# Row tile 11's normalised rows into a query-row buffer, and a new table of halved projections

## The chip, the core and the metric

The kernel runs on one core of a Trainium2 chip. The core has a matrix engine (PE, whose weight loads the profile lists apart as PEld), a vector engine (DVE), an activation engine (ACT), a general engine (POOL) and a queue engine (SP) that issues DMAs; POOL issues DMAs too. Each engine works through its own instructions in order and waits on semaphores for the others. Data lies in DRAM, in an on-chip buffer of 128 partitions (SBUF) and in the accumulators of the matrix engine (PSUM).

The metric is device time in microseconds (us) of one execution. The kernel before took 1621.09 us (median of 3 runs, 1619.76 to 1622.24).

## What is computed

Two layers, each applied twice in turn to the same 2048 rows of 512 values: a recurrent attention with a memory (A) and a gated mixer (B).

```python
x = x + A(layernorm(x)); x = x + B(layernorm(x))     # and both once more

# A: 64 segments of 32 rows, one after the other
h = concatenate([mem, xs])                 # 8 memory rows + 32 rows
q, k, v = h @ Wq, h @ Wk, h @ Wv           # 32 heads of 128
o = softmax(mask(q @ k.T * scale)) @ v @ Wo
mem = o[:8]                                # goes into the next segment
# B: over all 2048 rows
z = gelu(x @ w_in)                         # 1376 columns
g = w_sp @ layernorm(z[:, 688:]) + b_sp
out = (z[:, :688] * g) @ w_out
```

A segment needs the memory of the segment before it, so the 64 segments of a layer form one chain.

## The kernel before

**Blocks and segments.** The outer loop runs two blocks; each is `a_block` (64 segments, four to a row tile of 128 rows, 16 row tiles) and then `b_block`. `segment(s, ...)` issues one segment. On PE it holds, in this order: the projections of q and k in two halves each (`qk`, L929 and after), those of v (`v_mm`), the scores, the sums, the product with v, and the output projection with Wo (`wo_pairs`, L798; `wo_rest`, L805). Calls of `fill()` between them put in work that hangs on no recent result: the projections of the next row tile's last rows (`b_units`) or parts of an output projection (`y_part`, L817). A segment begins when DVE has written the new memory into the transposed rows `hT` (L907).

**Projections and their halving.** `mm_chunk` (L708 to L723) issues a projection of 512 columns as four contraction steps (`kt`) of four matmuls, one for each group of 32 partitions, each with its own weight load: 16 matmuls and 16 loads. While the counter `halve[0]` is above zero, a step with `kt > 0` is issued as two matmuls of 256 columns in place of one of 512, so 8 PE instructions more (4 loads and 4 matmuls), and the counter goes down by one. `segment` sets the counter behind the third q/k projection from the digit of `HALVED` that belongs to this block and segment (0 to 9); the fourth q/k projection and the two of v then use it up. What is computed stays the same. PE reads its program from DRAM in pieces, which the profile counts as the queue of instructions.

**Who orders what.** PE, DVE and ACT run in the order in which the code issues. The order on POOL in `a_block`, and that of SP there, is settled by a planner; in `b_block` SP is fixed as well and POOL is planned.

**The end of the attention.** Rows that have both their attention output and their residual are summed (`y_add`), their mean and variance taken (`y_stats`), and normalised by `y_norm` (L245 to L250): one DVE operation writes 512 bfloat16 columns into a buffer, and a DMA on SP stores it to `xb_d`, from which B loads transposed rows. Without a buffer as argument `y_norm` takes a tile `ln_xn`, a name with two buffers: the third user waits until the store that read the first has landed. At the end of `a_block` (L1260 to L1281) the row tiles 9 (in the last segment's `tail`), 10 and 11 are normalised one after the other (with `NB` = 16, `NB - 6` is 10 and `NB - 5` is 11). DVE's next operations are the two sums of `o_end` (L1277), the last attention output, stored by POOL (L1279) and SP (L1281).

**The start of the mixer.** `b_block` projects 16 row tiles (`project`, L296), with an activation on ACT (L297) and statistics on DVE (L300). DVE also adds the attention output to the row tiles 12 to 15 (`late_sum`, L228; its operands come by POOL, L222 and L224), takes their factors (`norms`) and normalises them (`late_norm`, L249). The first two of these take `ln_xn` again. POOL stores them to `xb_d` (L250), and SP loads them transposed (`load_rows`, L184) for `project(12)` and after. Then follow the 16 steps of the mixing product (L396) and of the output projection (L439), PE work throughout.

**The buffers of the query rows.** `segment` holds the projected q and k rows in tiles `rows` of the tag `rowsQK`, three buffers in the pool `rowp`; ACT writes them (L932), DVE transposes them (L935). Behind the last segment's transposes they lie idle. The pool ends with `a_block`, and its memory goes to tiles of `b_block`.

Of the kernel before, what the change touches and what calls it, by code (L numbers as in the profile page):

```python
# [7 lines left out]
BF16 = mybir.dt.bfloat16  # L8
# [6 lines left out]
P = 128  # L15
DM = 512
# [12 lines left out]
WO_PAIR = 18  # L29
LATE_STATS = 14  # L30
HALVED = (
    "5392919491949293909080707080708070807080708070708070807070807190",
    "8093929293929060070807070807080708070708070807080708070708070808",
)
OLD_SIZES = (H * P, 8 * DH, H * 32, H * 32)
ORDERED = {mybir.EngineType.PE, mybir.EngineType.DVE, mybir.EngineType.Activation}
# [451 lines left out]
def kernel(  # L488
# [57 lines left out]
    for blk in range(2):  # L546
        a_block(tc, c, rows, front, MV[0], RS[0], MV[1], RS[1], ahead, wo, S, first=(blk == 0))
        b_block(tc, c, rows, front, xd, MV[0], RS[0], B_w_sp, B_w_out, S, blk == 0, ahead, wo, out_final=out2 if blk == 1 else None)
# [114 lines left out]
def a_block(tc, c, rows, front, MV_in, RS_in, MV_out, RS_out, ahead, wo, S, first):  # L663
    nc = tc.nc
    NSEG = S // SEG
    NB = S // P
# [3 lines left out]
    with ExitStack() as ctx:  # L670
# [15 lines left out]
        rowp = ctx.enter_context(tc.tile_pool(name="a_rows", bufs=4))  # L686
# [70 lines left out]
        def run(todo):  # L757
            while todo:
                todo.pop(0)()
# [114 lines left out]
            if k == 2:  # L874
                copies.append(lambda: _rstd_act(nc, RS_in[:, tb:tb + 1], MV_in[:, tb, 1:2], c))

        def y_norm(tb, store):
            rows.y_norm(tb, MV_out[:, tb, 0:1], RS_out[:, tb:tb + 1], store)

        seg_state = {}  # L880
        oBs = {}
# [285 lines left out]
        for s in range(NSEG):  # L1167
            tb, j4 = s // 4, s % 4
# [62 lines left out]
            def tail():  # L1231
                if j4 == 1 + 2 * (first and tb == 0) and tb + 1 < NB:
                    spread_v(blk_state[tb + 1])
                if tb == NB - 1:
                    if j4 != 2:
                        front.load_w(j4)
                    if j4 > 0:
                        front.load_rows(j4 - 1)
                if ys and ys[0][1]:
                    y_norm(ys.pop(0)[0], nc.sync)  # L1240
                for y in ys:
                    y[1] = True
                if j4 == 0 and tb > 7 and (tb % 4 == 0 or tb == NB - 1):
                    due.extend(range(tb // 4 * 4 - 8, tb // 4 * 4 - 4) if tb < NB - 1 else range(NB - 8, NB - 4))
# [15 lines left out]
        for k in range(3):  # L1260
            y_stats(NB - 5, k)
        run(copies)
        for y in (NB - 6, NB - 5):
            y_norm(y, nc.sync)
        ends = (uT[NSEG % 2], oBs[NB // 4 - 1][:, :, 96:128])
        pw = accB.tile([P, 512], F32, name="pw")
        for n in range(H // 2):
# [51 lines left out]
```

## Time and profile before

| | |
|---|---|
| median of 3 runs | 1621.09 us (1619.76 to 1622.24) |
| profiled execution, its own time | 1622.86 us |
| its span, first to last instruction | 1621.2 us |
| instructions recorded | 94595 |
| granted PE clock, mean | 0.996 |
| busy DVE / ACT / POOL | 75% / 66% / 18% |
| DMA | 149.53 MB, 92 GB/s mean |

The profile is a page of one execution with views that can be asked of its trace. A row of the timeline gives the start in us from the span's start, the time covered, engine, source line, operation, output and input, the count, and in brackets how long the engine had been idle and what released it. The chain of waits follows the work that ended last backwards. A row of a stretch of time gives for each engine the busy time and the count, then the granted PE clock, the DMA share and GB/s.

### The profile page before, as it was taken

How to read it: one execution, taken by the hardware profiler on the slowest of the kernel's cores; microseconds unless marked ns; L12 is line 12 of the kernel's file. 1: busy time of each engine (PE TensorE's matmuls, PEld its weight loads, DVE VectorE, ACT ScalarE, POOL GpSimd, SP SyncE). 2: the span in 40 equal slices, each digit the busy share in tenths (PEclk: the TensorE clock that was granted, in tenths of full speed). 3: DMA queues.
4: the chain of work that ended last, by engine and by line, in shares of the span. 5: the costliest groups of instructions: out<-in, count | busy, mean ns of one | idle time of the engine just before them, and what ended most of it. 6: DMA issues, size and time to landing. Idle time of an engine off the chain costs nothing.

```text
span 1621.2 us, 94595 instructions
## 1 busy us (share of the span) xinstructions
PE 1571.4 (97%) x42719; PEld 1007.2 (62%) x42742; DVE 1208.3 (75%) x3169; ACT 1062.8 (66%) x2274; POOL 286.7 (18%) x604
## 2 busy tenths in 40 slices
PE   3899999999999999999999999999999999999999
PEld 1566666666666666666656666666667666665565
DVE  3677777778887887884477777777888788877622
ACT  2577777777777777761047777777777777776400
POOL 5111111112211221320011111111121112223000
PEclk9899999999999999999999999999999999999999
DMA  9322221223322345276962222222333233426596
GB/s 347 108 50 43 44 43 43 43 44 78 82 56 46 73 90 83 88 193 141 208 185 47 47 46 49 47 46 47 72 92 73 48 73 98 96 59 171 130 199 162
DMA packets 264764, 149.53 MB, mean 92 GB/s; under 512 B 198680, under 2 KB 240784, under 8 KB 264360
## 3 DMA queue, kind: packets, MB, share of 16 engines
q1 hardware_dynamic: 251128, 99.66, 29.2%
q0 software_dynamic: 13232, 43.82, 8.6%
q8 instruction: 335, 5.49, 1.5%
q14 instruction: 69, 0.57, 0.1%
HBM read 59.68 MB, written 37.19 MB: 60 GB/s over the span
## 4 chain that ended last, share of the span: by engine, by line
PE 92%; DMA 4%; DVE 1%; ACT 1%; issue 1%; POOL 0%; DVEq 0%; SPq 0%; POOLq 0%; ACTq 0%
PE psQ L721 14%; PE psK L721 14%; PE psb L721 9%; PE pg L396 9%; PE px L798 9%; PE psm L721 7%; PE psV L721 7%; PE psO L805 6%; PE pwB L817 3%; PE psO L1010 3%; PE pz L296 3%; PE py L439 2%; PE psT L1002 2%; PE psS L958 2%; DMA Wk_sb<-in_A_Wk_dram 1%; PE psO L1013 1%
## 5 line engine op out<-in xcount | busy, mean ns | idle before, releaser
L721 PEld LDWEIGHTS <-hT 128*32 128x32 bf16 x14404 | 380.3, 96 | 275.6 <-DVE hT L907 62.1
L935 DVE STREAM_TRANSPOSE QQ<-rows 128x512 bf16<-128x512 bf16 x256 | 179.6, 702 | 20.6 <-ACT rows L932 12.3
L935 DVE STREAM_TRANSPOSE KA<-rows 128x512 bf16<-128x512 bf16 x256 | 176.1, 688 | 14.2 <-ACT rows L932 13.5
L396 PE MATMUL pg<-z,wspT 128*128 128x344 bf16 x1024 | 154.3, 309 | 0.0
L932 ACT CAST rows<-psQ 128x512 bf16<-128x512 f32 x256 | 141.8, 584 | 18.2 <-PE psQ L721 17.2
L1032 DVE TENSOR_TENSOR uT<-psO,Rt 128x384 bf16<-128x384 f32 x256 | 141.4, 552 | 13.6 <-ACT Rt L1080 4.4
L1080 ACT ACTIVATE Rt<-Rt 128x512 f32<-128x512 f32 x256 | 147.3, 622 | 4.1
L1029 DVE TENSOR_TENSOR uT<-psO,Rm 128x128 bf16<-128x128 f32 x252 | 73.5, 292 | 96.7 <-ACT Rm L1028 50.7
L967 ACT ACTIVATE S<-psS 128x224 bf16<-128x224 f32 x256 | 91.4, 357 | 82.3 <-PE psS L962 82.2
L721 PE MATMUL psQ<-Wq_sb,hT 128*32 128x512 bf16 x2048 | 134.6, 381 | 7.5 <-ACT Rt L1077 5.1
L798 PEld LDWEIGHTS <-uT 128*32 128x32 bf16 x4608 | 111.6, 96 | 46.9 <-DVE uT L1029 31.6
L798 PE MATMUL px<-Wo,uT 128*32 128x256 bf16 x3840 | 135.4, 275 | 0.5 <-DVE uT L1029 0.5
L1077 ACT ACTIVATE Rt<-psT 128x1024 f32<-128x1024 f32 x128 | 131.0, 1024 | 5.5 <-PE psT L1002 2.5
L721 PE MATMUL psQ<-Wk_sb,hT 128*32 128x512 bf16 x2048 | 134.6, 381 | 0.0
L721 PE MATMUL psK<-Wk_sb,hT 128*32 128x256 bf16 (+1 forms) x2940 | 134.2, 314 | 0.0
L721 PE MATMUL psK<-Wv_sb,hT 128*32 128x256 bf16 (+1 forms) x2812 | 134.2, 321 | 0.0
L721 PE MATMUL psm<-Wq_sb,hT 128*32 128x512 bf16 x2048 | 134.2, 380 | 0.0
L721 PE MATMUL psV<-Wv_sb,hT 128*32 128x512 bf16 (+1 forms) x2508 | 133.7, 339 | 0.3 <-issue 0.3
L396 PEld LDWEIGHTS <-wspT 128*128 128x128 bf16 x1024 | 100.2, 98 | 53.2
L805 PE MATMUL psO<-Wo_high,uT 128*32 128x128 bf16 x7168 | 123.2, 219 | 2.3 <-DMA Wo_high<-in_A_Wo_dram 2.3
L890 POOL COPY KX<-old 128x128 bf16<-128x128 bf16 x128 | 68.3, 547 | 319.4 <-PE psS L962 242.9
L890 POOL COPY KX<-front 128x128 bf16<-128x128 bf16 x126 | 65.8, 543 | 304.3 <-PE psS L962 218.9
(196 smaller groups left out, 2896.9 us busy)
## 6 DMA issues: line engine op xcount, KB each, us to landing
o_d<-o_sb SPq DMA_DIRECT2D x126, 64.0 KB
vb_d<-front SPq DMA_DIRECT2D x30, 256.0 KB
VX<-vb_d SPq DMA_DIRECT2D x120, 64.0 KB
ln_x<-xd SPq DMA_DIRECT2D x26, 256.0 KB
y_o<-o_d POOLq DMA_DIRECT2D x22, 256.0 KB, 3.3
xd<-y_o POOLq DMA_DIRECT2D x22, 256.0 KB, 3.2
Wq_sb<-in_A_Wq_dram POOLq DMA_DIRECT2D x8, 512.0 KB, 10.1
Wk_sb<-in_A_Wk_dram POOLq DMA_DIRECT2D x8, 512.0 KB, 11.1
```

The source lines that it names most:

```text
L396: nc.tensor.matmul(pg[t][:, k, 0:344], lhsT=wsp[t][:, st, :], rhs=z(st, 344 * k, 344 * k + 344), start=(st == 0), stop=(st == NT - 1))
L721: mms.append(nc.tensor.matmul(ps[32 * cg:32 * cg + 32, n * k:n * k + n], lhsT=lhs(kt, cg), rhs=r[:, m * k:m * k + m], start=(kt == 0), sto ...
L798: nc.tensor.matmul(px[at:at + 32, 0:256], lhsT=lhs[:, h, :], rhs=wo_rhs(h, slice(k + 2, None, -2) if h % 2 else slice(k, None, 2)), start= ...
L805: nc.tensor.matmul(pw[32 * cg:32 * cg + 32, :], lhsT=lhs[:, h, :], rhs=wo_rhs(h, cg), start=False, stop=(h == H - 1), tile_position=(0, 32 ...
L890: eng.tensor_copy(KX[:, :, r].rearrange("p g (k i) -> p i g k", i=4), bs["KTB"][:, r].rearrange("p (i g) k -> p i g k", i=4)[:, :, :, 8 * ...
L932: return r, mms, nc.scalar.copy(r[:], ps)
L935: nc.vector.transpose(out=QQ[:, j % 2, :, 0:32] if j < 2 else KA[:, j % 2], in_=r[:])
L967: return nc.scalar.activation(out=S[:, r], in_=psS[:, r, 0:224], func=ACT.Exp, scale=scale)
L1029: nc.vector.tensor_tensor(out=hview(uT_cur[:], r, 24, 32), in0=oview(r, 0, 8), in1=rm.rearrange("p g (n q) -> p g n q", q=8), op=ALU.mult)
L1032: nc.vector.tensor_tensor(out=hview(uT_nxt[:], r, 0, 24), in0=oview(r, 8, 32), in1=rview(r, 0, 24), op=ALU.mult)
L1077: nc.scalar.activation(out=Rt[:], in_=psT[:], func=ACT.Ln)
L1080: nc.scalar.activation(out=rt, in_=rt, func=ACT.Exp, scale=-1.0)
```

## The change

Two edits. `y_norm` of `a_block` hands an optional buffer on, and row tile 11 is written to a tile `rows` of the tag `rowsQK` in place of `ln_xn`. And both strings of `HALVED` are replaced: the digits sum to 270 and 236 where they summed to 272 and 259. In the first block 15 digits differ, all of them among the segments 0 to 18 and 61 to 63. In the second nearly all do: before, the 7s and 8s stand at odd segments from 17 on, after at even ones, as they do in the first block in both versions.

```diff
 HALVED = (
-    "5392919491949293909080707080708070807080708070708070807070807190",
-    "8093929293929060070807070807080708070708070807080708070708070808",
+    "0385918690869077907080707080708070807080708070708070807070807084",
+    "6060030040859185918070807080707080707080708070807080708070708070",
 )
...
-        def y_norm(tb, store):
-            rows.y_norm(tb, MV_out[:, tb, 0:1], RS_out[:, tb:tb + 1], store)
+        def y_norm(tb, store, xn=None):
+            rows.y_norm(tb, MV_out[:, tb, 0:1], RS_out[:, tb:tb + 1], store, xn)
...
-        for y in (NB - 6, NB - 5):
-            y_norm(y, nc.sync)
+        y_norm(NB - 6, nc.sync)
+        y_norm(NB - 5, nc.sync, rowp.tile([P, DM], BF16, name="rows", tag="rowsQK", bufs=3)[:])
```

In the built program this moves more than the diff shows. PE has 200 instructions fewer out of some 85,500. DVE's instruction for row tile 11 no longer waits for a DMA, only for DVE and ACT. On POOL the planner puts the store of `o_end` (L1279) ahead of the loads of the attention output for the row tiles 12 to 15 (L224), where it stood behind the second of them (first block) or the first (second block, where it now also goes ahead of one load of the residual, L222); near the end of the second block's attention it also moves a copy of `QQ` (L887) ahead of a store, and a load of `y_x` (L222) and a store of row sums (L229) past the small copy `seen` (L1195). ACT's and DVE's orders are the same otherwise, and so is SP's.

## The prediction

> **What bounds the kernel now.** First the page: which engine fills the span, and where the chain of waits runs.
>
> ```profile
> span 1621.2 us, 94595 instructions
> PE 1571.4 (97%) x42719; PEld 1007.2 (62%) x42742; DVE 1208.3 (75%) x3169; ACT 1062.8 (66%) x2274; POOL 286.7 (18%) x604
> q8 instruction: 335, 5.49, 1.5%
> PE 92%; DMA 4%; DVE 1%; ACT 1%; issue 1%; POOL 0%; DVEq 0%; SPq 0%; POOLq 0%; ACTq 0%
> ```
>
> PE carries 92% of the chain, so only what makes PE wait, or gives it less to do, moves the time. DMA carries 4%; I looked for where. Then the chain at the two places where an attention ends and a mixer begins, first in the first block, then in the second.
>
> ```profile
> 693.54 0.97 PE pz L296 x4
> ...
> 704.94 26.69 PE pz L296 x201
> 731.63 0.44 PE pg L396 x3
> ```
>
> ```profile
> 1480.75 5.43 DMA xb_d<-ln_xn
> ...
> 1486.30 0.56 DVE ln_xn L249
> ...
> 1490.50 0.70 DVE y_o L228
> ...
> 1502.79 3.99 DMA xb_d<-ln_xn
> ...
> 1506.91 3.96 DMA front<-xb_d
> ...
> 1510.92 4.78 PE pz L296 x15
> ...
> 1515.80 6.27 PE pz L296 x32
> 1522.07 1.02 PE pg L396 x7
> ```
>
> In the first block PE projects without a break from 704.94 to 731.63. In the second the chain leaves PE at 1480.75 and comes back at 1510.92: a store of `ln_xn` lands, DVE normalises row tile 11, sums the four late row tiles, normalises them, POOL stores them, SP loads them transposed, and only then can PE project row tile 12. The timeline shows what PE loses.
>
> ```profile
> 697.97 0.61 DVE L249 TENSOR_SCALAR ln_xn<-y_o,MV,RS 128x512 bf16<-128x512 f32 x1 [2.63 <-DMA xb_d<-ln_xn]
> ...
> 1479.89 0.80 SPq L811 DMA_DIRECT2D o_d<-yB  x1
> ...
> 1481.58 0.20 ACT L121 ACTIVATE RS<-RS 128x1 f32<-128x1 f32 x1
> 1481.81 0.58 ACT L1274 COPY o_end<-pw 128x512 f32<-128x512 f32 x1
> ...
> 1483.71 2.53 ACT L297 ACTIVATE z<-pz 128x1376 bf16<-128x1376 f32 x2
> ...
> 1486.30 0.55 DVE L249 TENSOR_SCALAR ln_xn<-y_o,MV,RS 128x512 bf16<-128x512 f32 x1 [4.67 <-ACT z L297]
> 1486.88 1.40 DVE L1277 TENSOR_TENSOR o_end<-pw,o_end 32x512 f32<-32x512 f32 x2
> 1487.14 0.54 POOL L224 DMA_DIRECT2D y_o<-o_d  x1 [4.68 <-DVE ln_xn L249]
> ...
> 1494.22 9.24 PEld L296 LDWEIGHTS <-front 128*128 128x128 bf16 x48
> ...
> 1503.51 4.59 PEld L296 LDWEIGHTS <-ln_x 128*128 128x128 bf16 x24
> ...
> 1510.92 11.15 PE L296 MATMUL pz<-front 128*128 128x512 bf16 x47 [2.45 <-DMA front<-xb_d]
> ```
>
> PE stood still for 2.45 us before 1510.92. DVE's idle 4.67 us are put down to ACT, whose result it needs (`RS`) was ready at 1481.78; the chain names the true last one, the store. And the four projections after the stop took 11.15 us (1510.92 to 1522.07), where four earlier ones took 9.29 (1494.22 to 1503.51). The windows say why:
>
> ```profile
> 1505.00:1510.00 5.00, 3.47 (x19) 1.62 (x17) 4.74 (x16) 4.68 (x6) 0.00 (x0) 1.00 0.38 91
> 1510.00:1515.00 5.00, 4.08 (x14) 1.78 (x15) 4.64 (x20) 1.22 (x2) 0.00 (x0) 0.73 1.00 201
> ```
>
> The granted clock (third number from the right) falls from 1.00 to 0.73 right behind the stop. From 1522.07 on the chain is PE to the end, so stop and slow clock, 2.45 + 1.86 = 4.3 us, go into the time in full.
>
> **The buffer of row tile 11.** The instruction keeps its work (0.55 us) and its place; it loses one wait, for the store of row tile 9's `ln_xn`. Behind it on DVE stand the two sums of `o_end` and all the statistics of the mixer; POOL's load of `y_o` waits for it too, since that load overwrites what it reads. With the new buffer DVE starts row tile 11 at 1481.8 (`RS`), the sums at 1482.4 (ACT's copy ends at 1482.39) and the statistics of the first two projections when ACT has made them, 1485.0 and 1486.2. So DVE is free for the first late sum at about 1487.4; before, it was free at 1490.50, 3.1 later (from the end of the sums at 1486.88 + 1.40 the statistics took 2.2).
>
> What is late next is the late sum's operand, `y_o<-o_d`. POOL now issues the store of `o_end` first, after 1483.1 (1482.4 + one sum of 0.7), then one more load, 0.54 us each, then `y_o` at about 1484.5, 2.6 earlier than 1487.14. It also waits for the store of `yB`, issued at 1479.89; its neighbour, `xb_d` in the chain, took 5.43 us, which would make it 1485.3. How long the load takes is bounded by its own row and a neighbour's:
>
> ```profile
> xo<-xd POOLq DMA_DIRECT2D x1, 256.0 KB, 5.5
> y_o<-o_d POOLq DMA_DIRECT2D x1, 256.0 KB, 2.9
> ```
>
> 2.9 us gives 1487.4, 5.5 gives 1490.0. The same transfer is the nearer row, but it now falls among others, so I take 3.7: landing at 1488.2, DVE's late chain 2.3 us earlier, and everything behind it (norms, stores, transposes) as well, since from 1490.50 on DVE has no idle to give. PE's stop shrinks from 2.45 to about 0.15: **-2.3 us**, bounds -2.45 (all of it) and -0.5.
>
> The clock: the slow stretch follows a stop of 2.45 us. With 0.15 left I expect none: **-1.85 us**, bounds -1.86 and 0.
>
> In the first block DVE wins its 2.63 us too, but PE has no stop there to win back: 0. The store now reads a buffer of the attention's pool, whose memory the mixer takes over; the first users are `z` tiles of later projections, more than 10 us behind, and the store lands in 5.4: 0. `late_norm` now takes the buffers of row tiles 9 and 10 in place of 10 and 11, stored long before: 0. On POOL, the load of `y_x` that moves behind `seen` (0.2 us) feeds a sum a segment later: 0; without that cover, 0.2 us once.
>
> **The table.** A halved step costs 8 PE instructions more and hardly any time. By the first weight load of each segment, number 12 (9 halvings), then 22 (7) and 23 (none):
>
> ```profile
> 165.48 0.14 PEld L721 LDWEIGHTS <-hT 128*32 128x32 bf16 x8 [0.79 <-DVE hT L907]
> ...
> 175.51 0.13 PEld L721 LDWEIGHTS <-hT 128*32 128x32 bf16 x8 [0.30 <-DVE hT L907]
> ```
>
> ```profile
> 265.48 0.18 PEld L721 LDWEIGHTS <-hT 128*32 128x32 bf16 x8 [0.25 <-DVE hT L907]
> ...
> 270.67 0.37 PEld L958 LDWEIGHTS <-KA 128*32 128x32 bf16 x16
> ...
> 273.82 0.89 PEld L805 LDWEIGHTS <-uT 128*32 128x32 bf16 x56
> ...
> 275.50 0.18 PEld L721 LDWEIGHTS <-hT 128*32 128x32 bf16 x8 [0.25 <-DVE hT L907]
> 285.49 0.18 PEld L721 LDWEIGHTS <-hT 128*32 128x32 bf16 x8 [0.25 <-DVE hT L907]
> ```
>
> 10.03 us with 9 (segment 12), 10.02 with 7 (segment 22), 9.99 with none (segment 23): some 3 ns a halving. 25 fewer: **-0.1 us**.
>
> What the digits do move is where PE's program is fetched. 42719 + 42742 instructions in 335 packets of 16 KB are 255 to a packet: PE gets its code in pieces of 256, and a late piece stops it in the midst of independent work:
>
> ```profile
> 632.75 0.12 PEld L721 LDWEIGHTS <-hT 128*32 128x32 bf16 x6
> 633.61 0.44 PEld L721 LDWEIGHTS <-hT 128*32 128x32 bf16 x18 [0.74 <-issue]
> ```
>
> In the built order that load is number 194 past a multiple of 256, as are other such stops. A pair of a long and a short segment holds about 1280 instructions, five pieces, so the borders stay put from pair to pair. Counted from the start of a long segment they lie now near 0, 256, 512 and, in the short one, 98 and 354; with the new table near 34, 290, 546, and 130, 386. The densest piece was 256 to 512 (3.6 us by the rows of segment 22); it becomes 290 to 546, from the scores (270.67) into the output projection (just behind 273.82): 3.35 us. Segment 12 has its borders at 29, 285, 541, close to that, and takes 10.03. I charge 0.01 us to each of 57 long segments: **+0.6 us**. Bounds: all of PE's projection loads waited this long for issue, one such stop being 0.74:
>
> ```profile
>   issue: 10.8, 35
> ```
>
> If a third of it goes, -3.6; if each long segment loses half of the quarter microsecond by which its densest piece has shrunk, 57 x 0.13 = +7.4.
>
> The Trainium skill (Runtime: NRT & Kernel Launch, Instruction fetch mechanics) says that code comes in 16 KiB blocks of 256 instructions, which the packets bear out, and that the cost of crossing a block is mostly hidden, which the 0.74 us above does not. By the rule this term would be 0 and the forecast 0.6 us lower.
>
> **The sum.** -2.3 - 1.85 - 0.1 + 0.6 = -3.65 against the profiled execution's own 1622.86 us: 1619.2. That execution lies 1.77 over the median of the runs, 1621.09, and its span 1.66 under its time. Taken over to the median: **1617.4 us**.
>
> **Rivals.**
> - *No clock to win.* The execution profiled may owe its 1.77 us over the median to the slow clock, which the other runs then lack. For: the sizes agree (1.86). Against: runs spread by 2.5 us without any profile. 1621.09 - 2.3 + 0.5 = 1619.3. The Trainium skill (TensorE: Matmul & The Clock Gate, Why this matters for your kernels) lets the clock fall after gaps over about 3 us; the 2.45 us here sufficed.
> - *The operand takes the wait's place.* The load takes 5.5 us in the crowd; PE's stop shrinks by 0.5 only and the clock still falls: 1621.09 - 0.5 + 0.5 = 1621.1.
> - *Slower: the dense piece.* From a fetch of over 3.35 us on, each long segment stops in its output projection, where nothing covers it. At 0.13 us in 57 segments: 1617.4 - 0.6 + 7.4 = 1624.2; with all of the 0.25 us lost in each, 1631. For: the spare time lost. Against: segment 12.
> - *The new places help.* A third of the issue waits goes: 1617.4 - 0.6 - 3.6 = 1613.2. For: 10.8 us are there. Against: I see no border that moves out of a worse place.
> - *Nothing happens*, because another wait holds row tile 11: it waits for DVE and ACT alone, both done at 1481.8, so no more than the second rival's case.
>
> **How the numbers follow.** Forecast 0.45, no clock to win 0.12, operand 0.08, dense piece 0.18, new places 0.17; the last two get more than their rows say, since 57 segments repeat whatever a border costs or saves, and one profile shows few of the new places. The likeliest's own range is 1616 to 1619. The range takes in the first two rivals, half of the last and the lower edge of the dense piece: 1612.5 to 1623.5. This measurement can tell about 0.2% (3.2 us) from no change, so faster means under 1617.85: seven tenths of the forecast's case, the last rival, a quarter of the clock rival, 0.52. Slower means over 1624.3: three quarters of the dense piece and a little for what I haven't seen, 0.15. The rest, 0.33, is the same.
>
> **What would show it.** Right: DVE's row tile 11 near 1481.8 on the old scale with no idle before it, `y_o<-o_d` issued within 3 us of it, PE's stop before `project(12)` under 0.5 us, the window behind it at a clock of 1.00, four last projections in 9.3 us. Pairs of segments of 20.02 to 20.03 us show the table's price. Wrong: the stop still over 1 us, or long segments of 10.1 us and more with idle put down to issue inside the output projection.

## The result, and the profile after

The changed kernel took 1628.87 us (median of 12 runs, 1622.78 to 1634.26), the kernel before 1621.14 beside it (12 runs, 1618.68 to 1626.90): slower, ratio 1.0039, 95% interval 1.0025 to 1.0054. Measured again (`after_2` below) it took 1624.39, slower by the same ratio within the errors. The profiled execution took 1630.85 us. From its page:

```profile
span 1629.1 us, 94420 instructions
PE 1573.6 (97%) x42642; PEld 997.7 (61%) x42642; DVE 1207.6 (74%) x3169; ACT 1064.2 (65%) x2274; POOL 286.9 (18%) x604
q8 instruction: 334, 5.47, 1.4%
PE 90%; DMA 5%; DVE 2%; ACT 1%; issue 1%; POOL 0%; SPq 0%; DVEq 0%; POOLq 0%; ACTq 0%
```

PE has less of the chain (90%, 92% before), waits have more. Where the 7.9 us of span lie is read from the first weight load of certain segments, in both traces:

| stretch | before, us | after, us |
|---|---|---|
| first block, start of segment 0 to start of segment 63 | 645.90 | 645.96 |
| of it, segments 20 to 33 | 140.08 | 140.07 |
| segment 63, first mixer, to segment 0 of the second block | 154.09 | 153.94 |
| second block, segment 0 to segment 63 | 632.54 | 639.53 |
| of it, segments 51 to 62 | 121.55 | 127.75 |
| from the start of segment 63 of the second block to PE's last load | 151.77 | 153.26 |

Where nothing disturbs them, pairs of segments take what they took. In this execution the loss sits late in the second block. The largest single piece, segment 56 (13.54 us, 10.07 before), in the timeline of PE and in windows:

```profile
1400.60 0.56 PEld L721 LDWEIGHTS <-hT 128*32 128x32 bf16 x18
1404.32 0.10 PEld L721 LDWEIGHTS <-hT 128*32 128x32 bf16 x2 [3.16 <-issue]
```

```profile
1398.00:1400.00 2.00, 2.00 (x60) 1.34 (x53) 2.00 (x5) 1.32 (x3) 0.00 (x0) 1.00 1.21 121
1400.00:1402.00 2.00, 1.66 (x66) 1.04 (x54) 1.57 (x3) 1.27 (x3) 0.47 (x1) 1.00 0.73 90
1402.00:1404.00 2.00, 0.00 (x0) 0.00 (x0) 0.00 (x0) 0.00 (x0) 0.00 (x0) 1.00 0.14 38
```

PE's weight loads stop for 3.16 us in the midst of projections that wait for nothing; the reading is that it has no program. The load that resumes is number 194 past a multiple of 256 in the built order, as the forecast found for such stops. The DMA engines were full (share 1.21, then 0.73) and moved little (121, then 90 GB/s); the same stretch of the kernel before ran so:

```profile
1394.00:1396.00 2.00, 2.00 (x52) 0.99 (x44) 1.68 (x8) 1.95 (x4) 0.70 (x2) 1.00 0.88 208
1396.00:1398.00 2.00, 2.00 (x44) 0.99 (x40) 2.00 (x6) 1.45 (x3) 0.29 (x1) 1.00 1.22 244
```

In the records of the instruction queue the packet that was wanted began 5.34 us after PE had entered the piece before it (median over all packets 0.77 us), and PE went on 1.27 us after it had landed. Segment 58 loses 1.4 us in the same way.

The stop in segment 56 is itself one of a single execution. In the second profile of the changed kernel, `after_2`, this segment took 10.20 us, and in none of the 13 other profiles did a packet begin more than 3.7 us behind such an entry. Segment 58 stopped again:

```profile
1417.89 1.20 PEld L721 LDWEIGHTS <-hT 128*32 128x32 bf16 x28 [1.25 <-issue]
```

The second block up to segment 63 took 634.93 us there, 2.4 more than before.

Then the passage from attention to mixer. The timeline of DVE, POOL, SP and PE in the changed kernel's first profile (on the old scale 6.40 us less):

```profile
1486.18 0.53 DVE L249 TENSOR_SCALAR ln_xn<-rowsB,MV,RS 128x512 bf16<-128x512 f32 x1
...
1488.22 0.55 DVE L249 TENSOR_SCALAR rows<-y_o,MV,RS 128x512 bf16<-128x512 f32 x1 [0.19 <-ACT RS L121]
...
1489.80 0.52 POOL L1279 DMA_DIRECT2D o_d<-o_end  x1 [2.38 <-DVE o_end L1277]
...
1490.97 0.54 POOL L224 DMA_DIRECT2D y_o<-o_d  x1
1490.99 6.56 SPq L184 DMA_TRANSPOSE front<-xb_d  x2
...
1498.23 0.69 DVE L228 TENSOR_TENSOR y_o<-y_o,y_x 128x512 f32<-128x512 f32 x1 [4.39 <-DMA y_o<-o_d]
...
1504.55 0.69 DVE L228 TENSOR_TENSOR xo<-xo 128x512 f32<-128x512 f32 x1 [3.62 <-DMA xo<-o_d]
...
1504.67 1.67 PE L296 MATMUL pz<-front 128*128 128x512 bf16 x4 [3.74 <-DMA front<-xb_d]
```

```profile
y_o<-o_d POOLq DMA_DIRECT2D x1, 256.0 KB, 7.2
xo<-o_d POOLq DMA_DIRECT2D x1, 256.0 KB, 13.0
```

```profile
1505.00:1510.00 5.00, 5.00 (x19) 2.01 (x18) 4.79 (x11) 1.06 (x1) 1.44 (x3) 0.66 1.16 232
```

The wait is gone as foreseen: row tile 11 starts 2.04 us after row tile 9 (6.52 before), and `y_o` is issued 2.6 us earlier on the old scale. But the load takes 7.2 us in place of 2.9 and the next 13.0 in place of 3.6, so the late sums begin later than before. PE stops for 3.74 us, at another place (for the transposed rows of row tile 6), and the granted clock falls to 0.66 behind it.

In the 12 runs behind the median of 1628.87 the time goes with the mean granted clock (1622.78 to 1625.99 us in the five at 0.998, 1628.50 to 1634.26 in the seven at 0.992 to 0.997), in those of `after_2` hardly, so how much of the larger loss is a slow clock and not waiting stays open.

### The profile page after: what moved, and what is told of

Its sections match the earlier page's. It is cut to its first block, busy times and chain, and to the rows that moved or that the text cites. A ratio compares the mean times of both kernels' runs of the same rounds, so it can differ in the third digit from the quotient of the medians.

```text
span 1629.1 us, 94420 instructions
## 1 busy us (share of the span) xinstructions
PE 1573.6 (97%) x42642; PEld 997.7 (61%) x42642; DVE 1207.6 (74%) x3169; ACT 1064.2 (65%) x2274; POOL 286.9 (18%) x604
## 4 chain that ended last, share of the span: by engine, by line
PE 90%; DMA 5%; DVE 2%; ACT 1%; issue 1%; POOL 0%; SPq 0%; DVEq 0%; POOLq 0%; ACTq 0%
PE psQ L721 14%; PE psK L721 14%; PE psb L721 9%; PE pg L396 9%; PE px L798 9%; PE psm L721 7%; PE psV L721 6%; PE psO L805 6%; PE pwB L817 3%; PE psO L1010 3%; PE pz L296 3%; PE py L439 2%; PE psT L1002 2%; PE psS L958 2%; DMA Wk_sb<-in_A_Wk_dram 1%
## 5 line engine op out<-in xcount | busy, mean ns | idle before, releaser
L721 PEld LDWEIGHTS <-hT 128*32 128x32 bf16 x14312 | 371.8, 96 | 288.6 <-DVE hT L907 66.7
L721 PE MATMUL psK<-Wv_sb,hT 128*32 128x512 bf16 (+1 forms) x2836 | 133.9, 320 | 0.0
L805 PE MATMUL psO<-Wo_high,uT 128*32 128x128 bf16 x7168 | 124.4, 219 | 3.4 <-DMA Wo_high<-in_A_Wo_dram 2.3
```

The source lines that it names most:

```text
L721: mms.append(nc.tensor.matmul(ps[32 * cg:32 * cg + 32, n * k:n * k + n], lhsT=lhs(kt, cg), rhs=r[:, m * k:m * k + m], start=(kt == 0), sto ...
L805: nc.tensor.matmul(pw[32 * cg:32 * cg + 32, :], lhsT=lhs[:, h, :], rhs=wo_rhs(h, cg), start=False, stop=(h == H - 1), tile_position=(0, 32 ...
```

## The experiments

Each was timed beside the kernel before on the same chip; rows with the same time of before share a chip. All have 12 runs but `after_2` (11), `e_shift64` (6) and `e_shift128` (5). The last column is the mean of the runs less that of the kernel before, with the standard error of this difference; the medians and ratios are those of the comparison.

| kernel | median | before | ratio, 95% interval | means, difference |
|---|---|---|---|---|
| changed kernel | 1628.87 | 1621.14 | 1.0039 (1.0025 to 1.0054) | +6.1 ± 1.3 |
| after_2, the same again | 1624.39 | 1617.82 | 1.0034 (1.0022 to 1.0046) | +5.6 ± 0.9 |
| e_buf | 1620.66 | 1617.89 | 1.0012 (1.0001 to 1.0024) | +1.7 ± 0.8 |
| e_table | 1620.46 | 1617.89 | 1.0020 (1.0010 to 1.0030) | +2.6 ± 0.7 |
| e_old_shift | 1618.45 | 1617.89 | 1.0009 (0.9999 to 1.0019) | +0.8 ± 0.6 |
| e_new_shift | 1620.40 | 1617.89 | 1.0016 (1.0003 to 1.0028) | +2.5 ± 0.8 |
| e_hold | 1619.86 | 1617.82 | 1.0013 (1.0003 to 1.0023) | +1.8 ± 0.6 |
| e_shift64 | 1626.43 | 1617.82 | 1.0052 (1.0036 to 1.0067) | +8.2 ± 1.2 |
| e_shift128 | 1639.20 | 1617.82 | 1.0137 (1.0118 to 1.0155) | +22.2 ± 1.3 |
| e_shift16 | 1619.83 | 1617.86 | 1.0012 (1.0000 to 1.0025) | +1.4 ± 0.9 |
| e_new16 | 1620.69 | 1617.86 | 1.0017 (1.0005 to 1.0028) | +2.7 ± 0.8 |
| e_table_0 | 1618.47 | 1617.86 | 1.0011 (0.9999 to 1.0023) | +1.3 ± 0.8 |
| e_dve | 1619.14 | 1617.86 | 1.0005 (0.9994 to 1.0016) | +0.9 ± 0.7 |

### One edit at a time

`e_buf` is the changed kernel with the old table, `e_table` the kernel before with the new table.

> Only the buffer of row tile 11 is changed, the table of halved projections is that of before. Theory P (places): the loss sits in the places where PE's program is fetched, which this kernel has as before, so its time is that of before or up to 4 us less. Theory T (transfers): the earlier store of row tile 11 lets the transposed loads run into POOL's loads of the attention output; in the profile after, those loads took 7.2, 13.0 and 12.0 us (2.9, 3.6 and 3.1 before) and the tail behind the last segment's start took 153.26 us (151.77 before); then this kernel is 1 to 2 us slower than before, with loads of 7 us and more. Theory L (luck): the stalls of one profile fall anywhere; all four kernels stand within 2 us of one another.

> Only the table is changed, row tile 11 keeps the old buffer. P: the places of the fetches are those of the changed kernel (32, 290 and 546 in a long segment); slower than before by 5 to 8 us, with stops of PE put down to issue of 0.5 us and more in the segments 51 to 62 of the second block. T: the time of before, within 1 us. L: within 2 us of the others.

> The changed kernel once more, beside the others on this chip. If the two halves add up (1.7 us of mean for the buffer and 2.6 for the table in the runs before), it is 4 to 6 us slower than before. If the 7.7 us between the medians were mostly the chip of that day, 0 to 3 us.

Both edits cost, 1.7 and 2.6 us, and together 5.6 to 6.1: about what the halves add up to, though on different chips. Of the theories, T has the time and the long loads of `e_buf` (7.3 us, shown below), and P fails: its table was to cost 5 to 8 us, and its stops in the segments 51 to 62 are not in the profile of `e_table`, where no wait for issue in the second block's segments is over 0.6 us. L's condition is met by the four kernels `e_buf`, `e_table`, `e_old_shift` and `e_new_shift` (means 1618.5 to 1620.4), but not by the changed kernel.

In the profile of `e_table`, whose buffer is the old one, the passage to the second mixer reads:

```profile
1483.38 0.55 DVE L249 TENSOR_SCALAR ln_xn<-y_o,MV,RS 128x512 bf16<-128x512 f32 x1 [3.94 <-DMA xb_d<-ln_xn]
...
1507.88 6.33 PE L296 MATMUL pz<-front 128*128 128x512 bf16 x30 [1.60 <-DMA front<-xb_d]
```

```profile
1508.00:1513.00 5.00, 4.95 (x26) 2.48 (x26) 4.76 (x17) 2.06 (x3) 0.00 (x0) 1.00 1.12 201
```

DVE waits for the store (3.94 us), yet PE stops for 1.60 us only and the clock stays at 1.00. All profiles taken tell the same: with the old buffer PE's stops before row tile 12 were 2.45 (the profile of before), 1.60, 1.24, 0.39, 2.07, 0.47 and twice under 0.3 us (`e_table`, `e_old_shift`, `e_shift128`, `e_shift16`, `e_table_0`, `e_shift64`, `e_dve`), with a drop of the clock behind 2.45 and 2.07. With the new one they were 2.35, 0.99, 0.37 and 1.28 (`e_buf`, `e_new_shift`, `after_2`, `e_new16`), beside the 3.74 at the other place, and the clock fell behind 2.35 too. The stop that the forecast meant to win back in full belonged to the one execution that was profiled. Nor is the whole tail, from the start of segment 63 of the second block to PE's last load, clearly another: 148.02 to 152.50 us in the eight profiles with the old buffer, 147.93 to 153.26 in the five with the new one (means 149.53 and 150.25; without `e_hold`, where the transfers were moved as well).

### The places where PE's program is cut

```diff
-    "5392919491949293909080...     before
+    "1392919491949293909080...     e_old_shift: 32 instructions fewer
+    "3392919491949293909080...     e_shift16: 16 fewer
+    "0092919491949293909080...     e_shift64: 64 fewer
+    "0012919491949293909080...     e_shift128: 128 fewer
-    "0385918690869077907080...     changed kernel
+    "4385918690869077907080...     e_new_shift: 32 more (e_table_0: the same with the old buffer)
+    "2385918690869077907080...     e_new16: 16 more
```

> The kernel before with one digit changed: segment 0 of the first block has 1 halving in place of 5, so 32 PE instructions fewer, and from there to the end every piece of PE's program begins 32 instructions later in its segment (the places of the changed kernel, 32, 290, 546 and 130, 386), with the table otherwise as before. P: 4 to 8 us slower than before. T and a theory by which the digits themselves cost the time: the time of before within 1 us. L: within 2 us of the others.

> The changed kernel with one digit changed: segment 0 of the first block has 4 halvings in place of 0, so 32 PE instructions more, and every piece begins 32 instructions earlier in its segment, at the places of before (0, 256, 512 and 98, 354). Both edits stay. P: 5 to 8 us faster than the changed kernel (1628.87), so 1621 to 1624. T: 1622 to 1623, the tail still 153 us. A theory by which the digits cost the time: as slow as the changed kernel. L: within 2 us of the others.

> The kernel before with 8 halvings fewer in the segments 0 and 1 (0 and 0 in place of 5 and 3), so that every later piece of PE's program begins 64 instructions later in its segment: 65, 321, 577 in a long one, 162, 418 in a short one. Theory P (places): the time of the two blocks' late segments depends on these places by some us, so this kernel and the next differ from before, or from each other, by 1.5 us or more. Rival (the places do not matter): both within 0.7 us of before in the mean.

> The kernel before with 16 halvings fewer in the segments 0 to 2 (0, 0 and 1 in place of 5, 3 and 9): the pieces begin 128 instructions later, at 129, 385, 641 in a long segment and 226, 482 in a short one. P and rival as for the shift by 64.

A few halvings in the first three segments, which by themselves cost nothing that can be seen, move every later cut, and the time goes up by 8.2 and by 22.2 us. The waits of PE's weight loads (us in total, times, longest), first in the kernel before, then in `e_shift64`, in `e_shift128`, in the changed kernel and in `after_2`:

```profile
PEld L721 <- issue: 10.4, 34, 1.2
```

```profile
PEld L721 <- issue: 10.6, 35, 1.0
PEld L805 <- issue: 7.8, 18, 2.2
```

```profile
PEld L721 <- issue: 27.2, 65, 1.3
```

```profile
PEld L721 <- issue: 15.8, 35, 3.2
```

```profile
PEld L721 <- issue: 10.9, 32, 1.2
```

With the cuts 64 later PE stops in the output projection (L805: 18 waits; in the kernel before one, of 2.5 us, at the start), as the slower rival of the forecast had it for the new table's places; 128 later it stops 65 times, 16.8 us more than before, and many segments of the first block take 10.2 to 10.8 us where they took 9.94 to 10.08. In the changed kernel the sum grows by 5.4 us, of which the segments 56 and 58 make 4.6; in `after_2` it hardly grows. Laid over the weight loads of the profile of before (medians of four pairs of the first block), the five pieces of a pair take, in us:

| cuts moved by | pieces 1 to 5 | difference of means |
|---|---|---|
| 0 | 4.54, 3.59, 4.27, 4.30, 3.26 | 0 |
| 16 | 4.48, 3.48, 4.51, 4.03, 3.47 | +1.4 ± 0.9 |
| 32 | 4.46, 3.35, 4.80, 3.75, 3.66 | +0.8 ± 0.6 |
| 64 | 3.90, 3.26, 5.44, 3.49, 3.92 | +8.2 ± 1.2 |
| 128 | 2.98, 3.12, 5.77, 3.53, 4.61 | +22.2 ± 1.3 |

In the records of the instruction queue of the kernel before a packet begins 0.73 us (median) after PE has entered the piece before, takes some 1.1 us, and no piece was ever begun sooner than 1.19 us after its packet had landed: 3.0 us without any delay. By this sum pieces under that stop PE each time, and pieces of 3.26 inside PE's work stop it when the packet comes late. At 0 the piece of 3.26 ends where PE waits for the new memory anyway.

> The kernel before with 2 halvings fewer in segment 0 (3 in place of 5), so that the pieces of PE's program begin 16 instructions later: 17, 273, 529 in a long segment, 112, 368 in a short one. Laid over the weight loads of the profile of before (four pairs of segments of the first block), the shortest of the five pieces of a pair takes 3.26 us at the places of before, 3.47 at these, 3.35 at 32 later, 3.26 at 64 and 2.98 at 128. Theory P (a piece has to take longer than a fetch needs, some 3.3 us): no slower than before, -2 to +0.5 us in the mean, with fewer stops put down to issue. Rival (time rises with the distance from the places of before, whatever lies there): 0.3 to 2 us slower.

> The changed kernel, both edits, with 2 halvings in segment 0 (0 there), so that its pieces stand at the same places, 17, 273, 529 and 112, 368. P: the part of the table's loss that comes from the places goes, 5.6 over before becomes 1.5 to 3.5; what is left is the buffer's (1.7) and the digits'. If the digits cost and not the places: 4 to 6 over before.

> The new table with 4 halvings in segment 0, the old buffer, so the new digits at the places of before. The new table at its own places took 2.6 +- 0.7 over before (means), the old digits at those places 0.75 +- 0.56. P: within 1 us of before. If it is the digits (or the swap of long and short segments in the second block): 1.5 to 3 over before.

`e_shift16` was meant as a version that beats both, with its shortest piece at 3.47; it did not, and at 16 and 32 the differences are too small to be ordered. So P was wrong for `e_old_shift`, which was to lose 4 to 8 us at the new table's places and lost 0.8 ± 0.6. `e_new_shift` came just below P's 1621 to 1624, with a tail of 148.6 us and not T's 153. In the changed kernel the cuts seem to weigh more: moved from 34 to 18 its loss falls from 5.6 to 2.7, to 2.5 at 2, against kernels before on three chips. The new digits at the places of before cost 1.3 ± 0.8 (`e_table_0`), between the two expectations and not clear of noise. Which segments lose that isn't seen in its profile and stays open. That places can cost much is shown by the shifts of 64 and 128; how much of the table's 2.6 us is places and how much digits is not.

### The transfers at the passage

```diff
-            if tt % 2 == 1 and tt < 8:
+            if tt % 2 == 1 and 1 < tt < 8:
                 front.load_rows(tt // 2 + 3)
...
+            if tt == 1:
+                nc.vector.memset(front.take(KT * FF, 1), 0.0)
+                front.load_rows(3)
```

`e_hold` is `e_buf` with this; the second piece stands behind `late_sum(tt - 1)`.

> The table of before and the new buffer, but the transposed load of the row tiles 6 and 7, which the earlier store lets SP issue at 18.7 us after the last segment's start (22.0 to 23.2 with the old buffer), is held back until DVE has done the first late sum. Theory C (collision): in the new order that load runs beside POOL's load of y_o, which then takes 4.6 to 7.4 us (2.9 with the old buffer), so the late sums begin at 23.2 to 26.5 (23.5 to 24.7 with the old one). Held back, y_o lands within 3.5 us, the first late sum begins at 21.5 to 22.5, the four late row tiles are normalised before 34, PE stops under 1 us ahead of row tile 12, and the kernel is 1 to 3 us faster than the one with the buffer alone (mean 1.7 over before in the earlier runs), so that of before or 1 us less. Rival (POOL's load is slow because it meets the residual loads and stores that are under way at 18 us whatever SP does): the load still takes 4.5 us and more, and the time stays 1 to 2 us over before.

The rows of `e_buf`, whose last segment began at 1464.92, and then of `e_hold`, where it began at 1466.99 (its lines stand up to three further down), with the loads' times from issue to landing:

```profile
1483.64 6.53 SPq L184 DMA_TRANSPOSE front<-xb_d  x2
1484.01 0.54 POOL L224 DMA_DIRECT2D y_o<-o_d  x1 [0.53 <-DMA xb_d<-ln_xn]
...
1491.40 0.69 DVE L228 TENSOR_TENSOR y_o<-y_o,y_x 128x512 f32<-128x512 f32 x1 [4.93 <-DMA y_o<-o_d]
```

```profile
y_o<-o_d POOLq DMA_DIRECT2D x1, 256.0 KB, 7.3
```

```profile
1486.05 0.54 POOL L224 DMA_DIRECT2D y_o<-o_d  x1
...
1489.93 0.69 DVE L228 TENSOR_TENSOR y_o<-y_o,y_x 128x512 f32<-128x512 f32 x1 [0.92 <-DMA y_o<-o_d]
...
1491.67 2.69 SPq L184 DMA_TRANSPOSE front<-xb_d  x2
```

```profile
y_o<-o_d POOLq DMA_DIRECT2D x1, 256.0 KB, 3.8
```

In the kernel before, the first transposed load went out 23.20 us after the start of the last segment (1489.05 less 1465.85), since the stores of row tile 11 and of `o_end` stood ahead of it in SP's queue and waited for DVE. In the new order it goes out at 18.7, beside POOL's load. Held back, `y_o` lands in 3.8 us in place of 7.3, the late sum begins at 22.9 (26.5 in `e_buf`, 24.65 in the kernel before), and PE had no stop of 0.3 us before row tile 12. So the trace went nearly as theory C had it, all of it a little later than foreseen. The time did not: 1.8 ± 0.6 over before, as with the buffer alone, which is what the rival foresaw. In this one profile the attention of the second block took 634.57 us, 2.0 more than before, with the segments 51, 54 and 58 near 11 us. The edit also adds an instruction on DVE in each mixer, and the next section shows that this alone changes which segments are long, so its time is no clean test of the collision.

The longer load is in every profile: the load of `y_o` took 4.5 to 7.3 us in the five others with the new buffer, 2.9 to 3.9 in the eight with the old one. The first late sum began 23.2 to 26.5 us after the start of the last segment with the new buffer, 23.5 to 25.1 with the old (means 24.95 and 24.33): the start won on DVE was lost again on this load. That it makes the kernel slower is not shown.

### One instruction more on DVE

```diff
         for tt in range(NT):
+            if first and tt == 0:
+                nc.vector.memset(zp.tile([P, 1], F32, name="pad")[:], 0.0)
             project(tt)
```

With the new buffer the scheduler puts one wait more ahead of the statistics of the first mixer (L300), so that DVE's program from there on stands one place later. `e_dve` does that alone.

> The kernel before with one write of 128x1 added on DVE at the start of the first mixer, and nothing else: from there on every DVE instruction stands one place later in DVE's program, as it does with the new buffer, where the scheduler puts one wait more ahead of the statistics of that mixer. Theory D (part of the buffer's loss is that the borders of DVE's own program now fall on the instructions that write the new memory): segment 45 of the second block takes 10.14 to 10.16 us as in the profiles with the new buffer (9.93 to 9.95 in those without), by a start of the second memT 0.2 us later, and the segments 49 and 58 are 0.1 and 0.3 longer if they are of the same cause; in the mean 0.2 to 0.8 us over before. Rival (these segments are long because of what the buffer does to the transfers): segment 45 stays at 9.93 to 9.95.

| second block, us | 25 | 45 | 49 | 58 |
|---|---|---|---|---|
| e_table | 10.09 | 9.93 | 9.94 | 10.08 |
| e_old_shift | 10.09 | 9.95 | 9.95 | 10.05 |
| e_table_0 | 10.07 | 9.93 | 9.94 | 10.09 |
| e_buf | 10.31 | 10.16 | 10.09 | 10.37 |
| e_new_shift | 10.29 | 10.15 | 10.07 | 10.37 |
| e_new16 | 10.29 | 10.15 | 10.08 | 10.37 |
| e_dve | 10.33 | 10.16 | 10.09 | 10.35 |

The start of segment 45, first in the kernel before, then in `e_dve` (lines two further down):

```profile
1284.18 0.18 DVE L906 TENSOR_TENSOR memT<-psO,t 128x64 bf16<-128x64 f32 x1
1284.31 0.12 PEld L721 LDWEIGHTS <-hT 128*32 128x32 bf16 x8 [0.32 <-DVE hT L907]
1284.44 0.25 DVE L907 STREAM_TRANSPOSE hT<-memT 128x64 bf16<-128x64 bf16 x1
1284.74 3.81 PEld L721 LDWEIGHTS <-hT 128*32 128x32 bf16 x96 [0.31 <-DVE hT L907]
```

```profile
1282.83 0.12 PEld L723 LDWEIGHTS <-hT 128*32 128x32 bf16 x8 [0.17 <-DVE hT L909]
1282.92 0.22 DVE L908 TENSOR_TENSOR memT<-psO,t 128x64 bf16<-128x64 f32 x1
1283.18 0.24 DVE L909 STREAM_TRANSPOSE hT<-memT 128x64 bf16<-128x64 bf16 x1
...
1283.48 0.34 PEld L723 LDWEIGHTS <-hT 128*32 128x32 bf16 x12 [0.53 <-DVE hT L909]
```

The second `memT` starts 0.09 us behind PE's first load in place of 0.13 ahead of it, and PE waits 0.53 us in place of 0.31. The four segments together lose about 0.9 us (0.25 + 0.22 + 0.15 + 0.28, against the mean of the three upper rows), by one place in DVE's program and nothing else. The difference of means, 0.9 ± 0.7, agrees but is hardly clear of noise. The place decides, not the new buffer: in `e_hold`, which has that buffer and DVE's program two places later, 25 and 45 took 10.02 and 9.95 us, and 44 and 49 were long (10.42 and 10.30). Not every old profile fits as well as the three in the table: the kernel before had 10.27 in segment 25, for a reason not found, and `e_shift64` 10.24 and 10.25 in 45 and 49, with PE's cuts moved.

That DVE's own code is cut there, as PE's is, can be read from the traces. Counted from 0 with its waits, the instructions 2623, 3135, 3263 and 3519 of DVE, each 63 past a multiple of 128, fall in the four segments 25, 45, 49 and 58 of `e_dve` and begin late there. Behind each a packet of 8 KB, half of PE's 16 KB, begins 0.66 to 2.19 us later in the other queue of instructions. First 2623 and 3519 in `e_dve`, before which DVE idled 0.1 us or not at all in most other segments; then 3135 in `e_hold`, at the end of segment 44, where 0.04 us are usual:

```profile
1092.10 0.23 DVE L908 TENSOR_TENSOR memT<-psO,t 128x64 bf16<-128x64 f32 x1 [0.47 <-PE psO L807]
...
1423.51 0.29 DVE L901 TENSOR_TENSOR t<-px,cross 128x128 f32<-128x128 f32 x1 [0.46 <-DVE cross L898]
```

```profile
1283.17 0.25 DVE L910 STREAM_TRANSPOSE hT<-memT 128x64 bf16<-128x64 bf16 x1 [0.46 <-DVE memT L909]
```

## Why the prediction was wrong

The forecast was 1617.4, faster; measured were 1628.87 and 1624.39, both above the range too. The wait of row tile 11 went as foreseen; what was to follow from it did not.

- *"PE's stop shrinks from 2.45 to about 0.15: -2.3 us", and the clock's "-1.85 us"*: the first step that failed. Eight profiles with the old buffer put the stop between under 0.3 and 2.45 us and the drop of the clock in two of them; five with the new buffer have stops of 0.37 to 3.74 us, the longest ahead of row tile 6. A stop of one execution was taken for a property of the kernel. The rival "no clock to win" held half of this, with too small a chance.
- *"The same transfer is the nearer row ... so I take 3.7"*: the load of `y_o` took 7.2 us in the changed kernel and 7.3 in `e_buf`, 4.5 to 7.3 in all five profiles, in three of them above the upper bound of 5.5 that the rival on the operand used. So the late sums began on average no earlier. The forecast followed the freed wait on DVE and on POOL, but not on SP: the transposed loads behind the store in SP's queue came 4.5 us earlier too, into the load that was to be faster. With them held back (`e_hold`, one profile) the load took 3.8 us.
- *"In the first block ... 0"*: with the new buffer the stretch from segment 63 to the second block took 153.68 to 154.21 us in five profiles, 153.69 to 154.72 in eight with the old one; means 153.84 and 154.29. A gain of some 0.45 us there, if anything.
- *"The instruction keeps its work (0.55 us) and its place"*, priced at nothing: true of the instruction, not of those behind it. One wait more on DVE costs four segments of the next block 0.9 us.
- *The halvings, -0.1*: too small to be seen in any run.
- *"I charge 0.01 us to each of 57 long segments: +0.6"*: wrong in kind. Undisturbed segments pay nothing for the new places (140.08 and 140.07 us for 14 of them). The table costs 2.6 ± 0.7, and where is not seen: in the changed kernel two segments stopped for a late packet (3.16 and 1.46 us), in the segments of `e_table` none for over 0.6 us. The piece that the forecast called the densest (3.6) was not the shortest of before either, which is the fifth with 3.26.
- *The rival "slower: the dense piece"* had the sign, and its times (1624.2 to 1631) come nearest. Its mechanism, a stop where a piece is shorter than a fetch, is real when the cuts move by 64 and 128. At the places it spoke of it is not shown: `e_old_shift` has them and lost 0.8 ± 0.6, and the long stops of the changed kernel's profile fell in projections, not in the output projection. That its number came near is in part luck, since the buffer's loss is in the measured time.

The losses of the two edits, buffer 1.7 and table 2.6, make 4.3 ± 1.1 where 5.6 ± 0.9 were measured: the rest is within the errors. Of the buffer's 1.7 us, 0.9 ± 0.7 may be the place in DVE's program; what else it loses, and where the table loses its 2.6, stays open.

## What to carry to other kernels

A stall seen in one profile is a draw, not a price: before crediting its removal, look whether its length hangs on DMA timing and put its lower bound at zero. The same holds for a stall in the profile after. When a wait is removed, list what stands behind it in every queue, the DMA queue that stores the result first of all, and ask what those transfers will meet. On a kernel whose program is fetched in pieces, any edit moves the cuts of every later piece, on each engine whose count changes: compare the shortest piece with what a fetch takes, and try neutral shifts before judging the edit.

## What was not expected of the hardware

- A neutral shift of PE's program by 128 instructions costs 22.2 ± 1.3 us (1.4%).
- One instruction more on DVE lengthens four of 63 segments, 0.15 to 0.28 us each, the same four in all six profiles in which DVE's program stands one place later; two places later (`e_hold`) they are others.
- A packet of the instruction queue began 5.34 us after the piece before it had been entered, while the DMA engines were full at first (share 1.21, then 0.73) and moved 121, then 90 GB/s; PE's weight loads stood for 3.16 us. That happened in one of 14 profiles.
- The granted clock fell behind stops shorter than the 2.45 us that the forecast knew. In `e_shift16`:

```profile
1511.08 3.40 PE L296 MATMUL pz<-front 128*128 128x512 bf16 x9 [2.07 <-DMA front<-xb_d]
```

```profile
1511.00:1516.00 5.00, 4.87 (x16) 2.11 (x18) 4.69 (x18) 0.91 (x2) 0.00 (x0) 0.66 1.10 192
```

A stop of 2.07 us was followed by a clock of 0.66, one of 1.60 us (`e_table`) was not. Length alone does not decide: the matmuls of segment 56 in the changed kernel stood for 2.67 us, and the clock behind them stayed at 1.00.

```profile
1404.33 0.39 PE L721 MATMUL psV<-Wv_sb,hT 128*32 128x512 bf16 x2 [2.67 <-issue]
```

```profile
1404.32:1409.32 5.00, 4.81 (x186) 3.61 (x190) 3.04 (x9) 3.39 (x9) 1.03 (x2) 1.00 0.03 7
```
